# Attention block: scores from two fp32r parts with two heads side by side in 64-row halves, and dense work there in the same halves over three PSUM banks

## The chip, the cores and the metric

The kernel runs on one core of a Trainium2 chip. The metric is device microseconds of one execution. Engines are named as the profile names them: PE multiplies matrices, PEld loads its weights, ACT, DVE and POOL work element by element, and SP issues nearly all DMAs.

## The reference, cut

One transformer block on 2048 tokens of width 640: a layer norm, then attention (32 heads of 20, a sliding window of 256 keys) and a gated GELU MLP (1728 wide) side by side, summed with the input.

```python
xn = _layernorm(x)
q, k, v = qkv[0], qkv[1], qkv[2]            # qkv = xn @ wqkv, H = 32, Dh = 20
scores = einsum("bhqd,bhkd->bhqk", q, k) * Dh ** -0.5
mask = (i - j >= 0) & (i - j < 256)
p = softmax(where(mask, scores, -1e9)); o = einsum("bhqk,bhkd->bhqd", p, v)
A = o @ wo
B = (gelu(xn @ w_gate) * (xn @ w_up)) @ w_down
return x + A + B
```

## The kernel before

Weights and normalised inputs are split into a rounded part and a remainder, both fp32r, and a dense product is three passes over the five 128-row slices of the 640: 15 matmuls into one PSUM bank (`dense_steps`). The tokens are four chunks of 512.

**Prelude** (to some 60 us): layer norm, transposes, V of half the heads, and Q and K of the first tile of 128 columns. **Attention** (to some 565 us) is 32 units: `u` is a group of four heads and a chunk. **Then** come the rest of the gate and up products and the output products, in code that the change hardly touches.

A Q or K product of 128 columns and 512 tokens is one job of 15 matmuls. `save_qk` takes its bank apart into three bf16 parts: ACT rounds, DVE subtracts, ACT rounds the rest, POOL subtracts again, and `store` puts the tile `pt` into DRAM (`qd`, `kd`), in two or three DMAs of SP, one for each head group that the tile touches. `load_stack` brings a unit's parts back as six blocks of 20 rows for each head, 124 rows with four more that hold the row maximum and ones: `qs` and `ks`, 12 DMAs a unit.

A unit in attention has 14 slots (`NS`), in program order: 
- `max_pair`, eight a unit: scores of one block of queries for two heads, in bf16, on 60 rows in each of the two 64-row halves of the array and 32 output columns; DVE takes the row maximum. They come two at a time at the slots in `BURSTS` and behind the AV product.
- `max_end`: the negated maximum is turned (`ps_n`), ACT copies it to `mr`, and a DMA puts it into two rows of the query stack.
- `exp_piece`, twelve a unit (`SCORES`): for one head, the scores of up to 512 columns from the 124 rows, then one ACT exponential. `clear` masks them on POOL.
- `av_unit` at slot 0 of the next unit: probabilities times V in fp32, in 64-row halves and 32 columns, into two banks that ACT copies and POOL adds. `od` and `sd` take the result, five DMAs.
- Between them `pull_fill` draws 34.05 dense matmuls a unit (`RATE`) from `filler`: Q and K jobs of the tiles 1 to 4, V of the other heads, and gate and up products. Q and K jobs come in the units 0 to 10 and again in 18 to 21.

In this stage the order on PE, ACT, DVE, POOL and SP is the order of the code (`manual_schedule`). Work at later slots goes through `defer(n, fn)`, which puts it n slots on; `late` puts DVE work behind the slot's other work. SP issues its DMAs one by one, and each waits on one of eight semaphores in turn, that is, for the DMA eight places earlier to have landed. Eight PSUM banks: two for dense jobs (`psd`), six in a ring for scores, maxima and AV (`psr`).

Of the kernel before, what the change touches and what calls it, by code (L numbers as in the profile page):

```python
# [19 lines left out]
C = 512  # L20
# [9 lines left out]
QROWS = 64 + SR  # L30
NS = 14
BURSTS = 0, 4, 8
SCORES = {2: range(0, 3), 4: range(3, 5), 6: range(5, 7), 8: range(7, 9), 10: range(9, 12)}
# [6 lines left out]
KSLOT = 9  # L40
# [30 lines left out]
def block_kernel(ctx, tc, x, wqk, wv, wgu, wdo, wdl, out):  # L71
# [18 lines left out]
    qd = [dram.tile([NG, 3, 4 * DH, C], BF, name=f"qd{c}") for c in range(NC)]  # L90
    kd = [dram.tile([NG, 3, 4 * DH, C], BF, name=f"kd{c}") for c in range(NC)]
# [159 lines left out]
    def save_qk(t, c, ps):  # L251
        pt = qkp.tile([128, 3, C], BF, name="pt", tag="pt")
        r = qkp.tile([128, C], F32, name="r", tag="r", bufs=1)
        dst = (qd if t < 5 else kd)[c]
        h, l = (2, 0) if t < 5 else (0, 2)

        def lower():
            nc.scalar.activation(pt[:, 1, :], r, AF.Copy)  # L258
            nc.gpsimd.tensor_tensor(out=pt[:, l, :], in0=r, in1=pt[:, 1, :], op=OP.subtract)  # L259
            defer(2, store)  # L260

        def store():
            a, end = t % 5 * 128, t % 5 * 128 + 128
            while a < end:
                g, b = divmod(a, 4 * DH)
                n = min(4 * DH - b, end - a)
                p = n - end + a + 128
                nc.sync.dma_start(dst[g, :, b:b + n, :].rearrange("p m t -> m p t"), pt[p - n:p])
                a += n
            done.add((t, c))  # L270

        def middle():
            nc.vector.tensor_tensor(out=r, in0=ps, in1=pt[:, h, :], op=OP.subtract)
            defer(lag(), lower)

        def upper():
            nc.scalar.activation(pt[:, h, :], ps, AF.Copy)
            late(middle)

        defer(1, upper)  # L280
# [57 lines left out]
    NQ, NK = 3, 4  # L338
    qs = [st1.tile([128, 4, C], BF, name=f"qs{i}") for i in range(NQ)]
    ks = [st1.tile([128, 4, C], BF, name=f"ks{i}") for i in range(NK)]  # L340
    nms = [st1.tile([128, 4, 2, 4, 4], BF, name=f"nm{i}") for i in range(2)]
# [82 lines left out]
    with tc.tile_pool(name="lp", bufs=1, side="right") as lp:  # L424
# [15 lines left out]
        ones = lp.tile([4, 2 * C], BF, name="ones")  # L440
        nc.gpsimd.memset(ones, 0.0)
        nc.gpsimd.memset(ones[0:2], 1.0)
        for i in range(NK):
            for j in (0, 2):
                nc.sync.dma_start(ks[i][SR:64, j:j + 2].rearrange("p j t -> p (j t)"), ones)
        for c in range(1, NC):
# [13 lines left out]
            if c == 1:  # L460
                for i in range(NQ):
                    for j in (0, 2):
                        nc.sync.dma_start(qs[i][SR + 2:64, j:j + 2].rearrange("p j t -> p (j t)"), ones[2:4])
# [18 lines left out]
    psr = pp.enter_context(tc.tile_pool(name="psr", bufs=6, space=PSUM, reuse_waits="tile"))  # L482
    ap = pr.enter_context(tc.tile_pool(name="ap", bufs=2, side="right", reuse_waits="tile"))

    def load_stack(u, which=(0, 1)):
        g, c = divmod(u, NC)
        for m in range(80 * g // 128, (80 * g + 79) // 128 + 1):
            assert all((m + 5 * i, c) in done for i in which), (u, m)

        for i in which:  # L490
            dst, src, top, again = ((qs[u % NQ], qd[c], 1, 2), (ks[u % NK], kd[c], 0, 0))[i]
            for j in (0, 2):
                for p, part, n in ((j * 32, top, 2), (j * 32 + 2 * DH, again, 1), (64 - j * 32, 0, 3)):
                    nc.sync.dma_start(dst[p:p + DH * n, j:j + 2].rearrange("p j t -> p (j t)"),
                                      src[g, part:part + n].rearrange("s (d j) t -> (s d) (j t)",
                                                                      j=4)[:, j * C:(j + 2) * C])
# [6 lines left out]
    def max_pair(u, i):  # L503
        g, c = divmod(u, NC)
        jj, b = divmod(i, 4)
        q, k = qs[u % NQ], ks[u % NK]
# [5 lines left out]
        for h in range(4):  # L512
# [3 lines left out]
            if k0 < 0:  # L516
                parts.append((0, -k0, ks[(u - 1) % NK], C + k0, C) if c else (0, -k0, k, 0, None))
            todo += [(i_, h, q0, *part) for i_, part in enumerate(sorted(parts, key=lambda p: p[1] - p[0]))]
        for _, h, q0, lo, hi, kt, k0, k1 in sorted(todo, key=lambda p: p[:2]):
            for r, ps in enumerate(pss):  # L520
                rows, j = slice(64 * r, 64 * r + SR), 2 * r + jj
                keys = kt[rows, j, k0:k1] if k1 else kt[rows, j, 0:1].to_broadcast([SR, hi])
                nc.tensor.matmul(ps[32 * h:32 * h + 32, lo:hi], q[rows, j, q0:q0 + 32], keys,  # L523
# [6 lines left out]
        if i == 7:  # L530
# [4 lines left out]
            def negate():  # L535
                nc.vector.tensor_scalar(nm[:, 0, 0], mx, -1.0, None, op0=OP.mult)
                nc.vector.scalar_tensor_tensor(nm[:, 0, 1], mx, -1.0, nm[:, 0, 0], op0=OP.mult, op1=OP.subtract)
# [3 lines left out]
    def max_end(u):  # L541
        nm = maxes.pop(u)
        ps = bank("ps_n")
        nc.tensor.matmul(ps[:, 0:128], nm.rearrange("p z a j b -> p (z a j b)"), identb, start=True, stop=True)
        mr = ap.tile([32, 128], BF, name="mr", tag="mr")
        nc.scalar.activation(mr, ps[0:32, 0:128], AF.Copy)
        late(lambda: nc.scalar.dma_start(qs[u % NQ][SR:SR + 2].rearrange("p j t -> p (j t)"), mr))

    def pieces(c):
# [4 lines left out]
        return X, Z, Y  # L554
# [13 lines left out]
    def exp_piece(u, s):  # L568
        g, c = divmod(u, NC)
        bi, j = divmod(s, 4)  # L570
        todo = pieces(c)[bi]
        q = qs[u % NQ]
# [5 lines left out]
        ps = bank("ps_e")  # L578
        for kb, col, q0, n in sorted(todo, key=lambda p: p[3]):
            k = ks[(u - (kb < 4 * c)) % NK]  # L580
# [943 lines left out]
```

## Time and profile before

| | |
|---|---|
| time, three runs | 1043.07, 1043.63 (median), 1044.32 us |
| the profiled execution, its span | 1044.52 us, 1042.8 us |
| PE, DVE, ACT, POOL busy | 99%, 70%, 51%, 36% of the span |
| DMA moved | 158.95 MB, 152 GB/s on the mean |
| granted clock of PE | 0.999 |

All rows shown below are of this one execution. Matmuls overlap, so busy shares of PE say little of how fast it goes; distances between starts do. The start of the AV product marks a unit. SP's instructions are all issues and waits: the length of a row there is the time that SP took for the issue, not the transfer.

### The profile page before, as it was taken

Reading aid. Unit: us, or ns where it says so; the run is one execution under the profiler, and the core shown is the slowest. Engines: PE = TensorE matmul, PEld = TensorE weight load, DVE = VectorE, ACT = ScalarE, POOL = GpSimd, SP = SyncE. Lnnn points to the kernel's source line nnn. Section 1 sums busy time; section 2 is a strip of 40 time slices with the busy share of each in tenths; the row PEclk is TensorE's granted clock in tenths of the full one; section 3 lists DMA queues with packets and bytes.
Section 4 is the critical chain, followed back from the end, with each engine's and each line's share of the span. In section 5 each row is a group of like instructions: output and inputs, shape, how many; then the busy total and the mean of one; then the engine's idle time right before and its main releaser. Section 6 shows DMA issues by size and latency. Waiting matters only on the chain.

```text
span 1042.8 us, 28733 instructions
## 1 busy us (share of the span) xinstructions
PE 1027.2 (99%) x10941; PEld 853.3 (82%) x10941; DVE 728.3 (70%) x2007; ACT 527.8 (51%) x1120; POOL 377.1 (36%) x543
## 2 busy tenths in 40 slices
PE   8999999999999999999999999999999999999998
PEld 7987776677678876777677888888888999999998
DVE  8845666666665566776653778777556879888887
ACT  4444667666666667666666522323234544333332
POOL 5221778876565568665755111110110000000000
PEclk9999999999999999999999999999999999999999
DMA  5652465555333354444332557666216874443342
GB/s 201 190 148 62 134 180 162 171 158 175 104 105 93 94 168 135 150 126 142 100 92 91 190 187 248 232 240 243 102 66 248 257 234 137 136 128 119 119 137 92
DMA packets 105203, 158.95 MB, mean 152 GB/s; under 512 B 15420, under 2 KB 60092, under 8 KB 105064
## 3 DMA queue, kind: packets, MB, share of 16 engines
q1 hardware_dynamic: 102680, 150.95, 45.9%
q10 hardware_dynamic: 2384, 6.16, 1.9%
q8 instruction: 86, 1.41, 0.6%
q14 instruction: 53, 0.43, 0.1%
HBM read 101.78 MB, written 54.92 MB: 150 GB/s over the span
## 4 chain that ended last, share of the span: by engine, by line
PE 84%; DVE 7%; DMA 4%; ACT 2%; issue 1%; SPq 1%; POOL 0%; ACTq 0%; DVEq 0%
PE ps_d L110 22%; PE ps_g L968 21%; PE ps L1235 14%; PE ps_e L582 8%; PE ps_v L110 7%; PE ps_o L622 6%; PE ps_m L523 4%; DVE junk L527 2%; PE ps_g L110 1%; DVE ss L1073 1%; DMA qs<-qd 1%; DVE at L1073 1%; PE ps_t L181 1%; DVE wt L1073 1%; DMA stg<-wtd 1%
## 5 line engine op out<-in xcount | busy, mean ns | idle before, releaser
L527 DVE CUSTOM_DVE_ANT_0 junk<-ps_m,mask 128x288 bf16<-128x288 f32 (+2 forms) x512 | 227.8, 445 | 140.3 <-PE ps_m L523 82.5
L584 ACT ACTIVATE P<-ps_e 128x512 f32<-128x512 f32 (+2 forms) x384 | 195.5, 574 | 60.0 <-PE ps_e L582 58.9
L1235 PE MATMUL ps<-wb,at 128*128 128x320 f32 x999 | 156.4, 310 | 0.8 <-DVE xr L1261 0.7
L1235 PEld LDWEIGHTS ps<-wb,at 128*128 128x128 f32 x999 | 148.9, 188 | 1.4 <-issue 0.9
L595 POOL TENSOR_SCALAR_AFFINE_SELECT P<-P 128x512 f32<-128x512 f32 x128 | 83.8, 656 | 93.5 <-ACT P L584 92.2
L582 PE MATMUL ps_e<-qs,ks 124*128 124x128 bf16 (+2 forms) x704 | 107.3, 277 | 2.1 <-DVE mx L527 2.0
L110 PE MATMUL ps_d<-xh,wql 128*128 128x512 f32 x350 | 105.3, 410 | 0.0
L110 PE MATMUL ps_d<-xl,wqh 128*128 128x512 f32 x350 | 105.3, 410 | 0.0
L110 PE MATMUL ps_d<-xh,wqh 128*128 128x512 f32 x350 | 105.3, 411 | 0.0
L1235 PE MATMUL ps<-wt,at 128*128 128x320 f32 x552 | 89.3, 310 | 0.4 <-DVE u L1073 0.4
L582 PEld LDWEIGHTS <-ks 124*128 124x128 bf16 x704 | 51.5, 98 | 41.0 <-issue 24.0
L1235 PEld LDWEIGHTS ps<-wt,at 128*128 128x128 f32 x552 | 82.9, 188 | 0.9 <-DVE u L1073 0.9
L1189 ACT ACTIVATE at<-ss 128x512 fp32r<-128x512 f32 x59 | 37.3, 633 | 91.4 <-DVE ss L1073 91.4
L622 PE MATMUL ps_o<-P,v 64*32 64x320 f32 (+5 forms) x2816 | 82.0, 348 | 0.0
L103 POOL TENSOR_TENSOR wql<-wr,wqh 128x640 fp32r<-128x640 f32 x11 | 17.6, 1605 | 173.9 <-PE ps_g L968 129.4
L598 POOL TENSOR_SCALAR_AFFINE_SELECT P<-P 128x512 f32<-128x512 f32 x112 | 71.3, 647 | 16.9 <-ACT P L584 16.8
L622 PEld LDWEIGHTS ps_o<-P,v 64*32 64x32 f32 x2816 | 66.7, 106 | 9.8 <-DVE mx L527 4.5
L110 PEld LDWEIGHTS ps_d<-xh,wql 128*128 128x128 f32 x350 | 63.9, 189 | 12.8 <-issue 1.6
L110 PEld LDWEIGHTS ps_d<-xh,wqh 128*128 128x128 f32 x350 | 63.3, 189 | 12.6 <-issue 0.9
L110 PEld LDWEIGHTS ps_d<-xl,wqh 128*128 128x128 f32 x350 | 63.6, 189 | 12.1 <-issue 1.5
L523 PE MATMUL ps_m<-ks,qs 60*32 60x96 bf16 (+5 forms) x3008 | 64.9, 244 | 3.8 <-DVE mx L527 2.3
L259 POOL TENSOR_TENSOR pt<-r,pt 128x512 bf16<-128x512 f32 x40 | 46.8, 1170 | 57.4 <-ACT pt L258 57.4
(196 smaller groups left out, 1889.4 us busy)
## 6 DMA issues: line engine op xcount, KB each, us to landing
hr<-hd SPq DMA_DIRECT2D x104, 128.0 KB
hd<-he SPq DMA_DIRECT2D x50, 256.0 KB
wr<-wgu SPq DMA_DIRECT2D x27, 320.0 KB
qs<-qd SPq DMA_DIRECT2D x64, 120.0 KB
ks<-kd SPq DMA_DIRECT2D x64, 120.0 KB
xi<-x SPq DMA_DIRECT2D x16, 320.0 KB
qs<-qd SPq DMA_DIRECT2D x64, 80.0 KB
ks<-kd SPq DMA_DIRECT2D x64, 80.0 KB
```

Of the source, the lines that this page charges most:

```text
L110: nc.tensor.matmul(ps, a(k), b(k), start=n == 0, stop=n == 3 * nk - 1)
L259: nc.gpsimd.tensor_tensor(out=pt[:, l, :], in0=r, in1=pt[:, 1, :], op=OP.subtract)
L523: nc.tensor.matmul(ps[32 * h:32 * h + 32, lo:hi], q[rows, j, q0:q0 + 32], keys, start=True, stop=True, tile_position=(64 * r, 32 * h))
L527: nc.vector.tensor_tensor_reduce(out=junk[:, 0:n], in0=ps[:, 0:n], in1=mask[:, 288 - n:288], scale=1.0, scalar=NEG, op0=OP.add, op1=OP.max ...
L582: nc.tensor.matmul(ps[:, col:col + n], k[0:QROWS, j, kc:kc + 128], q[0:QROWS, j, q0:q0 + n], start=True, stop=True)
L584: nc.scalar.activation(pt[:, j, lo:hi], ps[:, lo:hi], AF.Exp, scale=SCALE)
L595: nc.gpsimd.affine_select(out=a, in_=a, pattern=[[0, 4], [1, 128]], compare_op=OP.is_ge, fill=0.0, base=0, channel_multiplier=-1)
L598: nc.gpsimd.affine_select(out=a, in_=a, pattern=[[0, 4], [-1, 128]], compare_op=OP.is_ge, fill=0.0, base=-1, channel_multiplier=1)
L622: nc.tensor.matmul(halves[h][32 * j:32 * j + 32, q0:q0 + n], v[rows, w0_:w0_ + 32], pts[u, bi][rows, j, col:col + n], start=i == 0, stop=i ...
L968: nc.tensor.matmul(ps, i, j, start=first and n == 0, stop=n == len(work) - 1, skip_group_check=True)
L1189: nc.scalar.activation(hi[:, 3:7], s, AF.Copy)
L1235: nc.tensor.matmul(ps[bank][:, 0:HD], *work[bank][j], start=bank not in begun, stop=final[p, bank] == n and j == len(work[bank]) - 1, skip ...
```

## The change

**Scores.** `save_qk` leaves two fp32r parts (tile `pe`: rounded, remainder) and two bf16 parts (tile `pm`), and both go to DRAM. A unit has two pairs of stacks: `qe`, `ke` in fp32r for the exponentials (three products of 20 rows and two rows for the maximum: 62 rows a head), `qm`, `km` in bf16 for the maxima (60 rows). Head `2r + j` lies in the half `r`, so one `exp_piece` multiplies two heads, one in each half, into two banks; there are six a unit, and 16 stack DMAs where 12 were. The maximum goes in by two DMAs on SP (one on ACT before).

**Dense work in attention.** A job is now 15 matmuls over the upper 64 rows, then 15 over the lower, into the same bank. `halves` runs the upper ones of one job beside the lower ones of the job before, over three banks (`psd`, `psd3`; the ring has five). Before a job's lower matmuls begin, a `nop` on ACT waits for its last upper one, and PE waits for the `nop`; six steps lie between (`HALF_LAG`).

**AV** uses all 128 rows and 32 columns and one bank, so one copy by ACT and no addition on POOL.

```diff
-BURSTS = 0, 4, 8
-SCORES = {2: range(0, 3), 4: range(3, 5), 6: range(5, 7), 8: range(7, 9), 10: range(9, 12)}
+BURSTS = 4, 8, 12
+SCORES = {1: (0,), 3: (1,), 5: (2,), 7: (3,), 9: (4,), 10: (5,)}
+HALF_LAG = 6
...
+    def soon(fn, *a):
+        if now[0] is None or now[0] < 0:
+            fn(*a)
+        else:
+            at(now[0] + 1, fn, *a)
...
     def save_qk(t, c, ps):
-        pt = qkp.tile([128, 3, C], BF, name="pt", tag="pt")
...
+        pe = qkp.tile([128, 2, C], F32R, name="pe", tag="pe")
+        pm = qkp.tile([128, 2, C], BF, name="pm", tag="pm")
...
-                nc.sync.dma_start(dst[g, :, b:b + n, :].rearrange("p m t -> m p t"), pt[p - n:p])
+                for d, part in zip(dst, (pe.bitcast(F32), pm)):
+                    nc.sync.dma_start(d[c][g, :, b:b + n, :].rearrange("p m t -> m p t"), part[p - n:p])
...
+        def third():
+            nc.gpsimd.tensor_tensor(out=pm[:, 1, :], in0=pe[:, 0, :].bitcast(F32), in1=pm[:, 0, :], op=OP.subtract)
+            defer(2, store)
+
+        def lower():
+            nc.vector.tensor_tensor(out=pe[:, 1, :], in0=ps, in1=pe[:, 0, :].bitcast(F32), op=OP.subtract)
 
         def upper():
-            nc.scalar.activation(pt[:, h, :], ps, AF.Copy)
-            late(middle)
-
+            nc.scalar.activation(pe[:, 0, :], ps, AF.Copy)
+            nc.scalar.activation(pm[:, 0, :], ps, AF.Copy)
+            late(lower)
+            defer(1, third)
+
+        soon(upper)
         defer(1, upper)
...
-        ps = bank("ps_e")
+        pss = [bank("ps_e") for _ in range(2)]
         for kb, col, q0, n in sorted(todo, key=lambda p: p[3]):
...
+            for r, ps in enumerate(pss):
+                rows = slice(64 * r, 64 * r + SR + 2)
+                nc.tensor.matmul(ps[:, col:col + n], k[rows, j, kc:kc + 128], q[rows, j, q0:q0 + n],
+                                 start=True, stop=True, tile_position=(64 * r, 0))
...
+                if n == len(up.steps):
+                    nop = nc.scalar.nop()
+                    tc.add_manual_dep(nop.ins, ins.ins.name, SYNC, reason="halves")
+                    second.append([up, nop.ins.name, HALF_LAG])
...
-                if u + 3 < NU and i in (KSLOT, 12):
-                    load_stack(u + 3, (int(i == KSLOT),))
+                if i == 1 and u + 2 < NU:
+                    load_stack(u + 2, 1)
+                if i == 2 and u + 1 < NU:
+                    load_stack(u + 1, 0)
```

`save_qk` ends in two calls for `upper`, the new one through `soon` and the old one through `defer`. From unit 0 on both put it one slot on; before that `soon` calls it at once. So all that hangs on `upper` stands in the program twice for each Q or K job.

On SP, before the change, at the end of unit 7's stretch: a Q job's three stores, and the stores of the attention result.

```order
L268 DMA qd_85<-pt 16x3x512 [waits DMAHW3_49,Pool_49]
L268 DMA qd_85<-pt 80x3x512 [waits DMAHW4_49]
L268 DMA qd_85<-pt 32x3x512 [waits DMAHW5_49]
L632 DMA od_95<-ob 20x512 [waits DMAHW6_49,Pool_49]
```

On SP, with the change, in the stretch of unit 6: the eight stores of one Q job with two pieces, a weight load, and the two DMAs of the maximum (`mr`). DMAHW0 to DMAHW7 are the eight semaphores of landed DMAs.

```order
L270 DMA qd_87<-pe 64x2x512 [waits DMAHW2_49,DVE_49,Activation_49]
L270 DMA qd_91<-pm 64x2x512 [waits DMAHW3_49,Activation_49,Pool_49]
L270 DMA qd_87<-pe 64x2x512 [waits DMAHW4_49]
L270 DMA qd_91<-pm 64x2x512 [waits DMAHW5_49]
L270 DMA qd_87<-pe 64x2x512 [waits DMAHW6_49,DMAHW2_49]
L270 DMA qd_91<-pm 64x2x512 [waits DMAHW7_49,DMAHW3_49]
L270 DMA qd_87<-pe 64x2x512 [waits DMAHW4_49,DMAHW0_49]
L270 DMA qd_91<-pm 64x2x512 [waits DMAHW5_49,DMAHW1_49]
L302 DMA wvr<-wv 128x320
L561 DMA qe_175<-mr 2x8x128 [waits Activation_49]
```

Where a two-piece job had two stores it now has eight; the last four write what the first four wrote, and each waits for the landing of the one four places earlier. The maximum of the next unit stands behind them.

On ACT, with the change, behind one AV product: the four exponentials of two score pieces, and then one job's bank is copied.

```order
L604 ACTIVATE P<-ps_e 128x512 [waits PE_49,Pool_49]
L604 ACTIVATE P<-ps_e 128x512 [waits PE_49] x3
L282 ACTIVATE pe<-ps_d 128x512 [waits DMAHW3_49,DMAHW1_49,DMAHW5_49,DVE_49,DMAHW7_49,PE_49,Pool_49]
L283 ACTIVATE pm<-ps_d 128x512 [waits DMAHW4_49,DMAHW6_49,DMAHW2_49,DMAHW0_49]
L282 ACTIVATE pe<-ps_d 128x512 [waits Activation_49]
L283 ACTIVATE pm<-ps_d 128x512 [waits Activation_49]
```

Four copies stand where `pt` had two activations (L277, L258); DVE and POOL have two subtractions each where they had one.

On PE, with the change, behind a burst of maxima: matmuls of two dense jobs alternate, one job's lower half (weights `wqh`, its first waits for ACT's `nop`) beside the next job's upper half (`wql`), and the scores of two heads.

```order
L731 MATMUL ps_d<-xh_77,wql 128x512
L731 MATMUL ps_d<-xh_77,wqh 128x512 [waits Activation_sequencer_49]
L731 MATMUL ps_d<-xh_77,wql 128x512
L731 MATMUL ps_d<-xh_77,wqh 128x512
L601 MATMUL ps_e<-qe_175,ke_177 128x128 [waits DMAHW3_49,DMAHW4_49,DMAHW0_49,DVE_49]
L601 MATMUL ps_e<-qe_175,ke_177 128x128 [waits DMAHW5_49,DMAHW6_49,DMAHW1_49,DVE_49]
L601 MATMUL ps_e<-qe_175,ke_178 128x384 [waits DMAHW7_49]
L601 MATMUL ps_e<-qe_175,ke_178 128x384 [waits DMAHW2_49]
```

The first scores of a unit wait for the landing of the stack loads and of the two DMAs from `mr`, all of them SP's now; before, ACT issued the one from `mr`.

SP's DMAs, counted in the two programs between one unit's `sd` store and the next:

| stretch | DMAs before | of them Q/K stores, stacks | DMAs after | of them Q/K stores, stacks, `mr` |
|---|---|---|---|---|
| units 1 to 10 | 247 | 55, 120 | 471 | 216, 160, 20 |
| units 18 to 21 | 91 | 16, 48 | 165 | 64, 64, 8 |
| units 11 to 17 | 130 | 0, 84 | 173 | 0, 112, 14 |

More of the change, by code (lines that the diff above doesn't have):

```diff
@@ L439, in block_kernel @@
         v0 = v0[0]
[L440 to L445, printed above, removed]
+        ones = lp.tile([2, C], F32, name="ones")
+        nc.gpsimd.memset(ones, 1.0)
+        for k in ke:
+            for r in (0, 64):
+                for j in range(2):
+                    nc.sync.dma_start(k[r + SR:r + SR + 2, j].bitcast(F32), ones)
         for c in range(1, NC):
@@ L505, in max_pair @@
         jj, b = divmod(i, 4)
[L506 removed]
+        q, k = qm[u % NQ], km[u % NK]
         if i == 0:
@@ L707, in filler @@
     def filler():
-        yield from proj_qk(0, w0, 3)
-        yield from proj_qk(5, w5, 3)
-        ws = [split_qk(raw) for raw in raws1]
+        yield from qk_job(0, w0, 3)
+        yield from qk_job(5, w5, 3)
+        ws = []
+        for t in range(8 + VEARLY, 12):
+            yield from v_job(v0, t)
+            ws.append(split_qk(raws1[len(ws)]))
         v1 = []
@@ L798, in block_kernel @@
     stream = ((u, i) for u in range(NU) for i in range(8))
-    fill = filler()
+    fill = halves(filler())
     debt = [0.0]
```

230 lines of the change are left out of this document (134 added, 96 removed).

## The prediction

> **What bounds the kernel now.** I read the page first, for the engine that is never idle and the chain that ended last.
>
> ```profile
> span 1042.8 us, 28733 instructions
> PE 1027.2 (99%) x10941; PEld 853.3 (82%) x10941; DVE 728.3 (70%) x2007; ACT 527.8 (51%) x1120; POOL 377.1 (36%) x543
> PE 84%; DVE 7%; DMA 4%; ACT 2%; issue 1%; SPq 1%; POOL 0%; ACTq 0%; DVEq 0%
> L622 PE MATMUL ps_o<-P,v 64*32 64x320 f32 (+5 forms) x2816 | 82.0, 348 | 0.0
> ```
>
> PE carries 84% of the chain. The L622 row shows that half-array matmuls do run side by side: 2816 of 348 ns are 980 us of length in 82.0 us. Only attention changes, so the chain of that window comes next, with the starts of four AV products, which mark units 0, 10, 17 and 21.
>
> ```profile
> by line: PE ps_d L110 42.1%; PE ps_e L582 17.5%; PE ps_o L622 12.3%; PE ps_m L523 8.3%; PE ps_v L110 7.8%; DVE junk L527 3.5%; DMA qs<-qd 2.7%; issue 1.5%; SPq L494 0.9%; SPq L268 0.6%; ACT P L584 0.5%; PE ps_n L544 0.4%; DVE nm L536 0.3%;
> ...
> 182.59 3.90 DMA qs<-qd
> ```
> ```profile
> 105.14 2.33 PE ps_o L622 x48
> ...
> 255.92 2.85 PE ps_o L622 x63
> ```
> ```profile
> 359.10 2.21 PE ps_o L622 x59
> 373.64 2.21 PE ps_o L622 x61
> ...
> 417.40 2.21 PE ps_o L622 x61
> ```
>
> Units 1 to 10 take 150.8 us, 18 to 21 take 58.3 us, a unit without Q and K jobs some 14.6 us (359.10 to 373.64). From 105 to 562.4 us the scores hold 17.5% of the chain, 80 us or 2.58 us for each of 31 units; AV 12.3%. But stack loads and SP's issues are on the chain too, so the last views are the windows and SP's own rows.
>
> ```profile
> core 0: us, PE busy (x) PEld busy (x) DVE busy (x) ACT busy (x) POOL busy (x), PEclk, DMA share, GB/s
> 105.10:255.90 150.80, 147.99 (x2384) 105.92 (x2375) 96.46 (x365) 102.67 (x206) 117.28 (x169) 1.00 0.56 161
> 359.10:417.40 58.30, 58.22 (x966) 42.02 (x963) 38.09 (x145) 39.85 (x81) 42.98 (x63) 1.00 0.49 141
> ```
> ```profile
> 236.23 1.31 SPq L268 DMA_DIRECT2D kd<-pt  x3
> 237.65 2.22 SPq L494 DMA_DIRECT2D ks<-kd  x6
> 239.96 1.33 SPq L268 DMA_DIRECT2D qd<-pt  x3
> 241.39 0.59 SPq L494 DMA_DIRECT2D qs<-qd  x1
> ```
> ```profile
> 229.99 1.42 SPq L632 DMA_DIRECT2D od<-ob  x4
> 231.46 0.50 SPq L633 DMA_DIRECT2D sd<-ob  x1
> ```
>
> Start to start, SP takes 1.42/3 = 0.47 us for a Q/K store, 2.31/6 = 0.385 for a stack load, 1.47/4 = 0.37 for an `od`, about 0.55 for an `sd`; I take 0.43, between them, for the others. The 247 DMAs of units 1 to 10 (55 stores, 120 loads, 40, 10, 22 others) then cost 26 + 46 + 15 + 5 + 9 = 101 us of 150.8. SP has a third of its time left, no more.
>
> **The change part by part.**
>
> *The doubled `upper`, and the stacks: SP.* Units 1 to 10 now have 471 DMAs: 216 stores, 160 loads, 20 from `mr`, 50 of AV, 25 others. An fp32r load and one from `mr` are not in the trace; both go by the load's 0.385. That is 102 + 62 + 8 + 20 + 11 = 203 us, more than the ten units take now. The queue is in order, and the next unit's scores wait for the two DMAs from `mr` that stand behind the stores: PE will wait there once a unit. Then the second store of a piece waits for the first to have landed, four to six stores (1.9 to 2.8 us) behind it. The load at 182.59 held the chain for 3.9 us; at that landing time each of some 22 jobs waits 1 to 2 us more, at 2 us it waits for nothing. I take 0.6 us: 14 us. Sum 217, **+66 us**. The nearest rows for the store's own price bound it:
>
> ```profile
> L268 SPq DMA_DIRECT2D qd<-pt x48: 316/436/1520, 22.9 to 413.9; - x48
> ```
>
> Some 40 ns lie between two issues (0.473 a store against the median 0.436). At the shortest, 0.316 + 0.04, it is 179 us without any landing wait (+28); at 0.52, a tenth above the two stretches, and with 2 us for each job 258 (+107). I stay by the two stretches above, which are what SP does back to back.
>
> Units 18 to 21: 64 stores, 64 loads, 8, 16, 4, 9: 30 + 25 + 3 + 6 + 2 + 4 = 70 us and 0.6 for each of 8 jobs, 75 against 58.3: **+17 us**, bounds +5 and +28. Units 11 to 17 with 25 DMAs, some 10 us a unit, stay PE's.
>
> *The doubled `upper`: the engines.*
>
> ```profile
> L277 ACT ACTIVATE pt<-ps_d x40: 577/597/632, 18.6 to 412.0; 128x512 bf16<-128x512 f32 x40
> L273 DVE TENSOR_TENSOR r<-ps_d,pt x40: 637/690/694, 20.3 to 414.8; 128x512 f32<-128x512 f32 x40
> ...
> L259 POOL TENSOR_TENSOR pt<-r,pt x40: 1157/1167/1332, 21.7 to 417.8; 128x512 bf16<-128x512 f32 x40
> ```
>
> A job had two ACT operations, one of DVE, one of POOL; it has four, two, two. With 2.25 jobs a unit this adds 2.7 us to ACT's 10.3 (102.67/10), 1.6 to DVE's 9.6 and 2.6 to POOL's 11.7; AV gives back one ACT copy and POOL's addition. All stay under 15 us a unit, SP's 21.7 hides them: nothing. Were SP not late, POOL would be next.
>
> *Scores and dense work.*
>
> ```profile
> 40.36 8.79 PE ps_v L110 x60
> 49.16 6.83 PE ps_d L110 x30
> ```
>
> An fp32r matmul takes 8.79/60 = 146.5 ns for 320 columns and 6.83/30 = 227.7 for 512: 0.423 ns a column and 11 ns each. Two heads side by side then take 11 + 11 + 512 × 0.423 = 239 ns for a piece, six pieces 1.43 us a unit against 2.58: −1.1. A 128-column matmul whose weights do not arrive in its 65 ns may give 0.15 of that back: −0.95 a unit. No row shows a dense matmul in halves. Two concurrent halves cost what the whole one costs, 227.7, or at best the bare columns, 217: 34.05 × 11 ns = −0.4 a unit; at worst they take turns (a rival below). I take 0, the nearest row.
>
> *AV and bursts.* AV had windows of up to 320 columns in halves, 1344 columns after one another in a full unit; now 1536: 1536/1344 × 2.21 = +0.3 us. Bursts of maxima now begin four times a unit from dense work, not three, and AV stands in a form of its own.
>
> ```profile
> 300.85 0.46 PE L110 MATMUL ps_v<-wvh,xh 128*128 128x320 f32 x2
> 301.23 0.45 PE L523 MATMUL ps_m<-ks,qs 60*32 60x32 bf16 x32
> ...
> 304.22 0.70 PE L110 MATMUL ps_v<-wvh,xh 128*128 128x320 f32 x3
> 304.76 0.74 PE L110 MATMUL ps_v<-wvh,xl 128*128 128x320 f32 x4
> ```
>
> Two matmuls before the burst should last 0.29 us; it starts 0.09 late. Behind it three take 0.54, 0.10 too long. So a burst costs 0.2, between 0 (if halves to halves is free, then −0.6 for the three that went) and 0.3. Behind this row stands a rule of the Trainium skill, "TensorEngine Tiling (Array Packing)", section "Key Properties": changing the tiling mode drains the array. The 0.09 and 0.10 agree; by it the change from AV's form to the maxima's drains once more, and the sum would be 17 × 0.2 = 3 us longer.
>
> A unit that PE bounds: −0.95 + 0.3 + 0.2 = −0.45, between −1.1 − 0.4 + 0.3 − 0.6 = −1.8 and −0.3; I take −0.6, as part of the 0.4 is likely. 17 such units (0, 11 to 17, 22 to 30): **−10 us**.
>
> *The staggering itself.* At the start 15 + 6 upper matmuls run alone, at the end as many lower ones: 42 × 0.228/2 = **+5 us**. The `nop` asks PE for nothing if ACT reaches it within six steps, 1.4 us; the exponentials are 574 ns each, so two may stand before it. Taken as nothing.
>
> *Prelude.* Six jobs do all twice, with 36 more DMAs, and the next chunk's loads of x stand behind the stores. PE is the chain there and the loads are early: **+3 us**, between 0 and 10.
>
> **Sum**: 66 + 17 − 10 + 5 + 3 = +81. The profiled execution took 1044.5 us, 1.7 more than its span; its time gives 1125.5, and the median shown is 0.9 under it: 1125.
>
> **Rivals.**
>
> *The DMA engines, not SP's issue.*
>
> ```profile
> qd<-pt SPq DMA_DIRECT2D x16, 240.0 KB
> ...
> qs<-qd SPq DMA_DIRECT2D x64, 40.0 KB
> ```
>
> 80 rows are 240 KB, a job 384 KB; twice two fp32 and two bf16 parts are 1536. Stacks go from 960 to 1440 KB a unit. Units 1 to 10 move 24.3 MB (161 GB/s × 150.8 us) and would move 56. At the full rate of that window, 161/0.56 = 288 GB/s, that is 195 us (+44), units 18 to 21 68 (+10): 1096. For it: near SP's 203. Against: SP's figure is higher. A rule of the Trainium skill, "DMA: Bandwidth & Descriptors", section "Issuing engines are not separate DMA queues", says that a sequencer's time for issuing is usually small beside the DMA itself; by it this rival is the case. The rows say otherwise: 101 us of issuing beside 0.56 × 150.8 = 84 us of transfers.
>
> *The `nop`.* If ACT is two exponentials late at each of 2.27 jobs, PE waits 2.27 × 1.15 = 2.6 us in 17 units that SP does not bound: +44, 1170. For it: ACT is in order, 70% busy; against: six steps of lead.
>
> *The halves take turns.* Then dense work costs 34.05 × 0.228 = 7.8 us more a unit; SP's wait covers that in 14 units, 17 pay 7.8: 1125 + 133 = 1258. Against: the L622 row.
>
> *Faster.* SP or the engines issue and move faster than any row, and PE's gain decides everywhere: at −1.2 a unit, the middle of −0.6 and −1.8, 31 units and the 8 of the last two parts give −29, 1015. It needs 47 DMAs and 5.6 MB in a unit of 13.4 us, 0.285 us a DMA and 418 GB/s. Against: the shortest issue is 0.316 for a store, and the fullest stretch gives 345 GB/s:
>
> ```profile
> 640.00:700.00 60.00, 60.00 (x267) 49.69 (x266) 47.18 (x80) 17.41 (x34) 8.96 (x6) 1.00 0.69 238
> ```
>
> **How the numbers follow.** SP 0.62, DMA engines 0.15, the `nop` 0.08, taking turns 0.04, faster 0.08, no change 0.03. 0.2% or 2 us is what a measurement can tell. The range 1068 to 1185 takes in SP's bounds nearly to their ends (1125 − 38 − 12, 1125 + 41 + 11 and the rest), the DMA engines and the `nop`; turns and faster lie outside. Slower 0.89.
>
> **What would show it.** In units 1 to 10 SP issues without a pause, PE waits once a unit for a DMA `qe<-mr`, and units take 20 us or more; units 11 to 17 take about 14. Wrong: a PE wait on `nop` in those, dense starts over 250 ns apart a pair, or units 1 to 10 under 18 us.

## The result, and the profile after

| | before | after |
|---|---|---|
| time, median (4 runs each, same chip) | 1043.35 us | 1303.14 us (1297.14 to 1308.19) |
| ratio, 95% interval | 1 | 1.2486 (1.2432 to 1.2541) |
| the profiled execution, its span | 1044.52, 1042.8 us | 1308.19, 1306.5 us |
| granted clock of PE | 0.999 | 0.926 |

The forecast was 1125 us, 1068 to 1185. The direction was right, the size was not: 264 us more of span, where 81 had been worked out.

The page of the changed kernel, the lines that answer to those of before; `PEclk` is the granted clock in tenths, for 40 slices of the span.

```profile
span 1306.5 us, 29772 instructions
PE 1125.5 (86%) x10885; PEld 903.8 (69%) x10885; DVE 752.0 (58%) x2047; ACT 552.9 (42%) x1200; POOL 379.3 (29%) x550
...
PEclk9886897778877889998889999999999999999999
...
PE 58%; DMA 14%; SPq 8%; DVE 8%; ACT 5%; issue 5%; POOL 2%; DVEq 0%; ACTq 0%; POOLq 0%
```

PE is no longer always busy (86%), and its share of the chain fell from 84% to 58%; DMA and SP's queue have 22% of it. The clock column tells where: most of its digits below 9 lie in the first half, at the start and where Q and K jobs run, and it is 9, its highest digit, elsewhere.

The starts of AV products in the chain of the changed kernel, which end units 10, 11, 18 and 22 (counted from 0), from three stretches of it; then the windows between such marks.

```profile
446.55 2.73 PE ps_o L629 x48
```
```profile
473.47 2.73 PE ps_o L629 x48
...
585.26 2.73 PE ps_o L629 x48
```
```profile
685.17 2.73 PE ps_o L629 x48
```
```profile
core 0: us, PE busy (x) PEld busy (x) DVE busy (x) ACT busy (x) POOL busy (x), PEclk, DMA share, GB/s
60.00:166.80 106.80, 83.46 (x731) 67.64 (x729) 37.69 (x120) 32.66 (x98) 27.38 (x35) 0.81 0.51 151
166.80:446.50 279.70, 187.83 (x2304) 127.65 (x2302) 109.49 (x386) 118.86 (x250) 130.31 (x179) 0.82 0.67 191
473.40:585.20 111.80, 107.48 (x1783) 79.86 (x1781) 63.12 (x248) 62.16 (x180) 52.31 (x90) 1.00 0.41 129
585.20:685.10 99.90, 73.15 (x924) 49.47 (x922) 43.12 (x154) 45.03 (x95) 46.79 (x67) 0.85 0.71 205
826.60:1306.50 479.90, 475.23 (x2696) 431.86 (x2695) 371.09 (x716) 177.65 (x323) 25.65 (x18) 1.00 0.52 171
```

The first AV product starts at 166.8 us for 105.0 before (+62). Units 1 to 10 take 279.7 us for 150.8 (+129), unit 11 26.9 for 15.1 (+12), 12 to 18, without Q and K jobs, 111.8 for 102.6 (+9), 19 to 22 99.9 for 58.3 (+42), 23 to 31 141.5 for 130.6 (+11), and all behind the last AV product 479.9 for 480.4. The sum is the 264 us. In the two stretches with Q and K jobs PE is busy for 187.83 of 279.70 and 73.15 of 99.90 us. These stretches run up to a unit behind the program's Q and K jobs (units 0 to 10 and 18 to 21), since SP still issues stores of them then: 9 in unit 11, 12 in unit 22.

One such unit, the one that begins with the AV product at 271.85 and with 34.9 us the longest of the ten: first SP's queue, then PE, in order of time (start, length, line, and in brackets the wait ahead), then the windows ahead of PE's pause, in it and behind it.

```profile
266.49 3.88 SPq L637 DMA_DIRECT2D od<-ob  x4
270.42 0.57 SPq L638 DMA_DIRECT2D sd<-ob  x1
271.09 0.61 SPq L270 DMA_DIRECT2D kd<-pe  x1
...
277.93 0.57 SPq L270 DMA_DIRECT2D kd<-pm  x1
278.62 0.57 SPq L270 DMA_DIRECT2D qd<-pe  x1
...
284.27 0.57 SPq L270 DMA_DIRECT2D qd<-pm  x1
284.90 0.60 SPq L302 DMA_DIRECT2D wvr<-wv  x1
285.56 1.41 SPq L561 DMA_DIRECT2D qe<-mr  x2
```
```profile
274.31 0.50 PE L731 MATMUL ps_d<-xl,wqh 64*128 64x512 f32 x1
...
274.65 0.39 PE L731 MATMUL ps_d<-xl,wqh 64*128 64x512 f32 x1
...
274.88 0.39 PE L731 MATMUL ps_d<-xl,wqh 64*128 64x512 f32 x1
274.88 0.39 PE L731 MATMUL ps_d<-xh,wql 64*128 64x512 f32 x1
287.95 1.24 PE L601 MATMUL ps_e<-qe,ke 62*128 62x128 f32 x4 [12.68 <-issue]
...
289.34 0.62 PE L731 MATMUL ps_d<-xl,wqh 64*128 64x512 f32 x1
...
289.76 0.62 PE L731 MATMUL ps_d<-xh,wqh 64*128 64x512 f32 x1
```
```profile
271.00:275.00 4.00, 4.00 (x78) 2.03 (x76) 1.60 (x8) 0.00 (x0) 0.00 (x0) 1.00 0.68 166
...
281.00:284.00 3.00, 0.00 (x0) 0.00 (x0) 1.19 (x2) 2.07 (x5) 1.16 (x2) 0.50 0.95 254
...
288.00:292.00 4.00, 4.00 (x20) 3.84 (x22) 0.00 (x0) 1.90 (x4) 0.00 (x0) 0.50 0.86 221
```

The two DMAs of the maximum stand behind sixteen stores of two jobs, eight of them the second time; the first scores start a microsecond behind them, after PE has stood for 12.68 us. It is the longest of 19 pauses of over 1 us in these ten units, 79 us together. ACT stood in this unit as well, for 10.69 us until 280.41: its copy into `pe`, a tile with two buffers, waits for stores out of it to land. PE's last wait is the one for the maximum; a third buffer was not tried. From 271.09 to 284.90 us are 13.81 for sixteen stores, 0.86 each. Behind the pause the same dense matmuls take 0.62 us and start 0.42 apart, ahead of it 0.39 and 0.23: the granted clock has fallen from 1.00 to 0.50. The Trainium skill, "TensorE: Matmul & The Clock Gate", Part 1, says that an idle array is taken to half its clock and back after about 3.4 us of work; the rows agree with the fall to half. The 0.82 of the ten units is the mean over many such pauses. The clock was still full when this pause began, so here the fall follows from the wait and is not its cause.

### The profile page after: what moved, and what is told of

Its sections match the earlier page's. It is cut to its first block, busy times and chain, and to the rows that moved or that the text cites. A ratio compares the mean times of both kernels' runs of the same rounds, so it can differ in the third digit from the quotient of the medians.

```text
span 1306.5 us, 29772 instructions
## 1 busy us (share of the span) xinstructions
PE 1125.5 (86%) x10885; PEld 903.8 (69%) x10885; DVE 752.0 (58%) x2047; ACT 552.9 (42%) x1200; POOL 379.3 (29%) x550
## 4 chain that ended last, share of the span: by engine, by line
PE 58%; DMA 14%; SPq 8%; DVE 8%; ACT 5%; issue 5%; POOL 2%; DVEq 0%; ACTq 0%; POOLq 0%
PE ps L1313 14%; PE ps_g L1046 14%; PE ps_d L731 12%; SPq L270 4%; PE ps_o L629 4%; PE ps_e L601 4%; DMA ke<-kd 3%; PE ps_v L731 3%; SPq L500 3%; PE ps_m L529 3%; DVE junk L533 2%; DMA kd<-pm 2%; DMA qd<-pm 2%; ACT pm L283 2%; PE ps_v L111 2%
## 5 line engine op out<-in xcount | busy, mean ns | idle before, releaser
L731 PE MATMUL ps_d<-xl,wqh 64*128 64x512 f32 x660 | 222.9, 442 | 0.0
L731 PE MATMUL ps_d<-xh,wqh 64*128 64x512 f32 x660 | 220.0, 445 | 3.3 <-DVE pe L279 3.3
L731 PE MATMUL ps_d<-xh,wql 64*128 64x512 f32 x660 | 222.6, 443 | 0.0
L601 PE MATMUL ps_e<-qe,ke 62*128 62x128 f32 (+2 forms) x704 | 117.4, 350 | 96.2 <-DMA qe<-mr 46.3
L601 PEld LDWEIGHTS ps_e<-qe,ke 62*128 62x128 f32 x704 | 89.9, 211 | 121.7 <-issue 77.2
L275 POOL TENSOR_TENSOR pm<-pe,pm 128x512 bf16<-128x512 f32 x80 | 93.2, 1166 | 221.0 <-ACT pm L283 152.0
L731 PEld LDWEIGHTS ps_d<-xh,wqh 64*128 64x128 f32 x660 | 129.6, 211 | 15.9 <-issue 4.6
L731 PEld LDWEIGHTS ps_d<-xh,wql 64*128 64x128 f32 x660 | 130.9, 211 | 13.0 <-issue 5.0
L731 PEld LDWEIGHTS ps_d<-xl,wqh 64*128 64x128 f32 x660 | 130.6, 210 | 11.5 <-issue 2.8
L629 PE MATMUL ps_o<-P,v 128*32 128x384 f32 (+2 forms) x1408 | 84.3, 386 | 0.0
```

The lines of the kernel that those rows point to most:

```text
L275: nc.gpsimd.tensor_tensor(out=pm[:, 1, :], in0=pe[:, 0, :].bitcast(F32), in1=pm[:, 0, :], op=OP.subtract)
L601: nc.tensor.matmul(ps[:, col:col + n], k[rows, j, kc:kc + 128], q[rows, j, q0:q0 + n], start=True, stop=True, tile_position=(64 * r, 0))
L629: nc.tensor.matmul(o[32 * j:32 * j + 32, q0:q0 + n], v[:, w0_:w0_ + 32], pt[:, j, col:col + n], start=i == 0, stop=i == len(todo) - 1, ski ...
L731: return nc.tensor.matmul(self.ps[:, 0:self.n], a[p, k, self.rows], b[p, k, self.cols], start=r == 0 and i == 0, stop=r == 1 and i == len( ...
```

## The experiments

Theory D: the doubled `upper` costs nearly all. Its rivals: the doubled work of ACT, DVE and POOL (E) and not the DMAs; bytes and not the number of DMAs; the new form of scores, AV and dense work itself (R). All kernels below are edits of the changed one, unless said otherwise. The stages in the table are distances between starts of AV products, from each kernel's trace; SP's DMAs are those issued in units 1 to 11, "us each" those units' time over that number. The times of the changed kernel, x1, c3 and b1 are medians of 4, 4, 4 and 6 runs; the others ran once, so differences of a few us between them say nothing (x1's four runs lie within 4.6 us, those of the changed kernel within 11).

| kernel | time | first AV | 1-11, a unit | SP's DMAs | us each | 12-18, a unit | 19-22, a unit |
|---|---|---|---|---|---|---|---|
| before | 1043.4 | 105.0 | 15.08 | 269 | 0.62 | 14.66 | 14.58 |
| after | 1303.1 | 166.8 | 27.87 | 507 | 0.60 | 15.97 | 24.97 |
| x1_once | 1159.1 | 123.7 | 20.72 | 391 | 0.58 | 15.83 | 18.62 |
| x2_engines_twice | 1179.0 | 142.1 | 20.83 | 391 | 0.59 | 15.96 | 18.43 |
| x3_stores_twice | 1273.8 | 142.1 | 27.06 | 507 | 0.59 | 15.81 | 25.20 |
| x4_stores_elsewhere | 1270.8 | 141.6 | 27.05 | 508 | 0.59 | 15.81 | 24.38 |
| x5_stores_small | 1249.4 | 135.3 | 26.28 | 507 | 0.57 | 15.84 | 23.03 |
| z1_one_result_store | 1140.4 | 123.6 | 18.29 | 347 | 0.58 | 15.73 | 16.93 |
| c1_turn_one_store | 1139.6 | 122.7 | 18.38 | 347 | 0.58 | 15.71 | 16.80 |
| p1_loads_on_pool | 1139.7 | 121.9 | 19.75 | 348 | 0.62 | 15.87 | 17.08 |
| c3_turn_store_pool | 1132.8 | 124.5 | 17.92 | 303 | 0.65 | 15.74 | 16.35 |
| m1_max_on_act | 1167.1 | 124.6 | 21.05 | 360 | 0.64 | 15.97 | 18.95 |
| y2_stacks_on_act | 1215.3 | 127.4 | 20.78 | 308 | 0.74 | 19.36 | 21.82 |
| y3_best | 1226.4 | 129.2 | 20.82 | 283 | 0.81 | 19.94 | 21.42 |
| w1_dense_whole | 1168.0 | 115.4 | 20.54 | 394 | 0.57 | 17.21 | 18.25 |
| v1_av_halves | 1162.0 | 124.8 | 20.74 | 391 | 0.58 | 16.07 | 18.65 |
| c2_all_whole | 1160.4 | 115.5 | 18.65 | 349 | 0.59 | 17.11 | 17.38 |
| y1_turn_whole | 1154.7 | 122.1 | 20.56 | 391 | 0.58 | 15.80 | 18.43 |
| b2_before_twice | 1141.8 | 132.3 | 20.06 | 330 | 0.67 | 14.79 | 18.38 |
| b1_before_one_store | 1060.5 | 104.9 | 14.99 | 226 | 0.73 | 14.65 | 14.63 |

### One `upper`

```diff
         soon(upper)
-        defer(1, upper)
```

> One `upper` a job instead of two; all else as changed. If the doubling is what costs (theory D), the time falls to about 1085 us, 1075 to 1095: the time before, plus 1.2 us for each of 31 units, which is what the changed kernel's units without Q and K jobs take more than before (15.4 to 16.5 us against some 14.6), plus some 5 us of start. If the forecast's small terms hold in all units it is 1040 us. If the new form of scores, AV and dense work is what costs (rival R), the time stays over 1200 us.

It took 1159.11 us (1157.59 to 1162.19, 4 runs), ratio 1.1109 (1.108 to 1.1137). So 144 of the 260 us are the doubling's (theory D), and 115 stay with the form (R); the 1085 us of D fails too, since I had carried the units without Q and K jobs over to those with them.

```profile
core 0: us, PE busy (x) PEld busy (x) DVE busy (x) ACT busy (x) POOL busy (x), PEclk, DMA share, GB/s
...
123.70:331.00 207.30, 169.79 (x2300) 113.57 (x2298) 95.78 (x364) 97.39 (x206) 105.27 (x158) 0.92 0.61 179
367.90:462.40 94.50, 91.67 (x1552) 69.11 (x1550) 50.51 (x209) 53.12 (x159) 41.14 (x69) 1.00 0.43 131
```

In these windows of it PE still waits in units 1 to 10 (169.79 of 207.30 us) and hardly in those without Q and K jobs (91.67 of 94.50). Even one set of stores leaves SP more than it had.

### Engines, stores, landings, bytes

The doubled half each way: all of `upper` twice but one `store` (x2); one `upper` and `store` twice, into one place (x3), the second into a place of its own (x4), and that with 128 of the 512 columns (x5).

```diff
 # x2
-        soon(upper)
-        defer(1, upper)
+        soon(upper, False)
+        defer(1, upper, True)        # True: third goes on to store
 # x3, x4, x5: one upper
-        defer(1, upper)
 # x3
             defer(2, store)
+            defer(2, store)
 # x4
+            defer(2, store, qx if t < 5 else kx)
 # x5
+                    w = C if dst in (qd, kd) else 128
```

> Both calls of `upper` stay, but only the second one stores: ACT, DVE and POOL do all twice, the DMAs are those of one call. If SP's issues and the landings of the stores are what costs, it lies within 25 us of the kernel with one `upper`, near 1100 us. If the doubled work of the engines costs (rival E), it stays at 1250 us or more.

> One `upper` a job, and `store` twice into the same place: ACT, DVE and POOL do everything once, the DMAs are those of the changed kernel and each second one waits for the landing of the first. If SP and the landings cost (forecast), units 1 to 10 take 25 us and more and the whole 1250 to 1300 us. If the engines cost (rival E), it is near 1100 us.

> As the kernel that stores twice, but the second time into a place of its own that nobody reads: the same number of issues and bytes, and no store waits for another to land. If the waits for landings make the difference between SP's pure issue time and what was seen, units 1 to 10 take 5 to 8 us less each than with both stores into one place, some 20 to 22 us, and the whole about 1180 us. If the issues or the bytes alone cost, the time is that of the kernel that stores twice, within 20 us.

> One `upper`; the second stores go to a place of their own and carry 128 of the 512 columns: as many DMAs and rows as where both stores are whole (1270.8 us), a quarter of the second ones' bytes. If the number of DMAs that SP has to issue costs, it stays at 1240 us or more. If the bytes on the DMA engines cost, a quarter of the 112 us between 1159 and 1271 is left: about 1187 us.

Measured: 1178.97, 1273.78, 1270.83 and 1249.42 us. In attention the doubled work of the engines costs nothing (20.83 us a unit for 20.72), and the doubled stores everything (27.06). Their landings cost next to nothing: with a place of its own for the second store the units are as long (27.05), so the wait of a second store for the first is not the term, which leaves the second of x4's two cases. Three quarters of the second stores' bytes taken away give 0.8 us a unit and 21 us in all; their number, with a quarter of the bytes and as many rows, keeps 90 of the 112 us. In the windows of x3 and x5:

```profile
60.00:142.10 82.10, 67.34 (x676) 53.47 (x674) 31.92 (x113) 24.04 (x72) 19.18 (x28) 0.85 0.59 171
142.10:413.60 271.50, 185.04 (x2300) 126.56 (x2298) 93.26 (x364) 97.96 (x206) 104.73 (x157) 0.81 0.69 196
```
```profile
135.30:399.90 264.60, 185.16 (x2303) 126.20 (x2301) 93.12 (x364) 97.92 (x206) 105.11 (x157) 0.81 0.54 155
```

The DMA engines go from 0.69 to 0.54 busy and from 196 to 155 GB/s, and the ten units from 271.5 to 264.6 us. The issue of a second store gets shorter too (`qx<-pe`, median, from 0.64 us in x4 to 0.44 in x5), so the length of an issue is not free of the bytes behind it.

Ahead of the first AV product both halves of the doubling cost, and as much: 123.7 becomes 142.1 with the engines' and 142.1 with the stores'; together 166.8. PE is idle for 15 and 14 of 82 us in the windows of x3, above, and of x2:

```profile
60.00:142.10 82.10, 67.92 (x659) 54.67 (x657) 28.17 (x97) 27.66 (x79) 20.30 (x21) 0.81 0.37 110
```

### Fewer DMAs for SP, by three ways

With one `upper`: one result store of 128 rows for five (z1); the same with one product that turns the maxima (c1); the bf16 loads on ACT (y2); the maximum's two DMAs on ACT (m1); the four bf16 query loads on POOL (p1), and that on c1 (c3). The edits of z1, c1 and c3 also read the result from its new place behind attention.

```diff
 # z1, c1, c3
-            for j in range(4):
-                nc.sync.dma_start(od[c].rearrange("(d h) t -> h d t", h=H)[4 * g + j], ob[32 * j:32 * j + DH, :])
-            nc.sync.dma_start(sd[c][4 * g:4 * g + 4, :], ob[DH::32, :])
+            nc.sync.dma_start(o2[c][128 * g:128 * g + 128], ob)
 # y2
-                    nc.sync.dma_start(to[64 * r + p:64 * r + p + DH * n].rearrange("p j t -> p (j t)"),
+                    (nc.sync, nc.scalar)[i].dma_start(to[64 * r + p:64 * r + p + DH * n].rearrange("p j t -> p (j t)"),
 # m1
-                nc.sync.dma_start(qe[u % NQ][64 * r + SR:64 * r + SR + 2]      # ...
+                nc.scalar.dma_start(qe[u % NQ][64 * r + SR:64 * r + SR + 2]    # ...
 # p1, c3
-                    nc.sync.dma_start(to[64 * r + p:64 * r + p + DH * n]    # ...
+                    (nc.gpsimd if any(dst is q_ for q_ in qm) else nc.sync).dma_start(to[64 * r + p:64 * r + p + DH * n]    # ...
```

> One `upper`, and the result of a unit goes to DRAM in one DMA of 128 rows where it took five, with about as many bytes (256 KB for 176); the reads of it much later take a few DMAs more. SP has 32 DMAs a unit with Q and K jobs where it had 36. If SP's queue bounds these units, by 0.58 us a DMA, they take 2 us less each: units 1 to 10 some 18.5 us, the whole about 1132 us. If bytes bound them, the time stays at 1159 or rises.

> One `upper`, the maxima turned by one product into one bank, one result store a unit. The sum of the two edits alone: 4.5 us and whatever the one store gives, by SP's queue 27 us: about 1128 us.

> One `upper`, and the eight bf16 stack loads of a unit are issued by ACT, so that SP has 8 of its 36 DMAs of a unit with Q and K jobs less; bytes and numbers of DMAs as a whole are the same. If SP's queue bounds units 1 to 10, they go from 20.7 us to about 17, and the whole to some 1115 us. If the DMA engines bound them, the time stays within 8 us of 1159. If ACT's own order makes it late, units without Q and K jobs get longer than 15.7 us.

> One `upper`, and the two DMAs of the maximum are issued by ACT as the one before the change was. By the count alone (34 DMAs a unit for 36, 0.58 us each) units 1 to 11 go from 20.7 to 19.5 us, the whole to about 1142. If these two standing behind the stores is what costs (order in the queue, not length), units 1 to 11 fall to 17 us or less, the whole under 1115.

> One `upper`, and the four bf16 query loads of a unit are issued by POOL: 36 DMAs in all as before, 32 of them on SP. If SP's queue bounds units 1 to 11 (0.58 us for each of its DMAs), they take 18.4 us for 20.7 as with one result store, the whole about 1125 us. If the DMAs as a whole bound them, or their landings, they stay at 20.7. If POOL gets late by issuing, units without Q and K jobs get longer than 15.8 us as with the loads on ACT.

> One `upper`, the maxima turned in one product, one result store a unit, and the four bf16 query loads on POOL: 28 DMAs a unit on SP. By 0.58 us a DMA units 1 to 11 take 16.2 us, near what PE needs (15.7), the whole about 1112 us, still slower than before the change. If something else than SP's queue bounds them, they stay above 18 us.

Taken away, four DMAs a unit are worth 2.4 us, as the rate of 0.58 us a DMA says (z1: 18.29 for 20.72, though the one store has 128 rows for 84; in all 1140.42 us and not 1132, because the product behind attention takes 17 us longer when it reads the new place). The turn in one product adds nothing to that (c1: 1139.62, expected about 1128). Given to another engine they are worth less. POOL, in the rows of p1, issues a load in 0.517 us and has room for it:

```profile
L499 POOL DMA_DIRECT2D qm<-qd x128: 510/517/683, 60.2 to 616.0; - x128
L499 SPq DMA_DIRECT2D km<-kd x128: 272/331/1286, 61.8 to 616.6; - x128
```

but the units fell by 1.0 us and not by 2.4, and the issues that stayed on SP in units 1 to 11 grew from 0.445 us on the mean (x1, without `qm`) to 0.469. So the rate seems to be SP's for one part and that of all DMAs together for another. The Trainium skill, "DMA: Bandwidth & Descriptors", "Issuing engines are not separate DMA queues", says that issuing on several engines saves only the sequencer's time; here it saved 1.0 of 2.4 us. On ACT nothing is gained at all. SP's waits from 100 to 380 us of m1:

```profile
SPq L636 <- DMA qe<-mr: 15.2, 8, 3.0
...
SPq L637 <- DMA qe<-mr: 6.1, 3, 4.8
SPq L499 <- DMA qe<-mr: 4.3, 1, 4.3
```

ACT issues the maximum when its own order lets it, and SP, whose later DMAs wait on the same eight semaphores, now waits for these landings: what was issue time is waiting, 67 us in units 1 to 11 for x1's 45. It also answers whether the two DMAs cost by standing behind the stores: without them there the units stay at 21.05 us. y2 shows the same on ACT's side, with 19.4 us in units that had been 15.8: its expectation's third case. y3 joins the edits of y1 (below), y2 and m1. It was expected at 1090 us by SP's queue or within 15 us of 1159 by the DMA engines, and took 1226.41: neither.

Counted over all engines that issue, units 1 to 11 have 391 DMAs in x1, 382 in m1, 396 in y2, 393 in y3 and 392 in p1, and take 217 to 232 us in all five; they have 347 in z1, c1 and c3, and take 197 to 202. That is 0.55 to 0.61 us a DMA, whoever issues it. So the number of DMAs sets the time of these units to within a tenth. That it does so by SP's issuing, and not by something that all DMAs share, is not shown.

c3 took 1132.79 us (1129.93 to 1135.9, 4 runs), ratio 1.0819 (1.0771 to 1.0867): the best of this form, and still slower than before.

### The form of dense work, AV and the turn

With one `upper`: dense jobs of 15 matmuls on all rows in turn (w1), that on c1 (c2), AV as before the change (v1), the maxima turned by one product into one bank (y1).

```diff
 # w1, c2
-    fill = halves(filler())
+    fill = whole(filler())        # a[:, k, rows], b[:, k, cols], one job after another
 # y1
-        pss = [bank("ps_n") for _ in range(2)]
...
+        ps = bank("ps_n")
+        nc.tensor.matmul(ps[:, 0:128], nm, identb, start=True, stop=True)
+        nc.scalar.activation(mr.rearrange("p r t -> p (r t)"), ps[0:32, 0:128], AF.Copy)
```

> One `upper`, and the negated maxima are turned by one product on all 128 rows into one bank, with one copy by ACT, where two products on 64 rows went into two of the ring's five banks. In the units that PE bounds, 0.65 us lie between the turn and the scores behind it; if that is the wait for a bank, some 0.4 us of it go in each of these 17 units: 8 us less, about 1151 us. If it is the wait for something else, nothing changes.

> One `upper`, and the dense jobs in attention are 15 matmuls on all 128 rows again, each into one of the three banks, with no `nop` and no staggering; scores and maxima stay in halves. If dense work in halves costs nothing by itself and saves a change of form at each piece of scores and each burst (10 a unit at 0.2 us), the units that PE bounds get up to 2 us longer than 15.7. If the halves and their banks are what costs, they fall towards 14.6. By both, the 5 us of the staggered start go. The Q and K units, which SP's queue bounds, stay at 20.7 us by my theory.

> The same with dense work on all 128 rows. In the units without Q and K jobs: the one before plus what dense work in whole rows gives or takes there, between 14.6 and 17.5 us a unit; in units 1 to 10, bound by SP's queue, no difference from the one before.

> One `upper`, and AV as in the kernel before: 64-row halves in two banks, two copies by ACT, the sum on POOL. If AV on 128 rows is what makes the units that PE bounds long (2.73 us for 2.21, and two changes of form), units 12 to 18 fall from 15.8 to 15.1 to 15.3 us and the whole to about 1150. If it is not, they stay at 15.8 or more. In units 1 to 11 no difference.

Dense work in halves is a gain: without it units 12 to 18 take 17.21 us for 15.83 (c2: 17.11), though the start is 8 us shorter (115.4 for 123.7). PE's waits ahead of weight loads in these units, first of w1, then of x1 (sum, times, longest, in us):

```profile
PEld L528 <- issue: 5.0, 19, 0.4
PEld ps_v L878 <- issue: 5.0, 25, 0.2
PEld ps_o L628 <- issue: 4.0, 20, 0.4
PEld ps_e L600 <- issue: 3.8, 18, 0.4
```
```profile
PEld L528 <- issue: 7.7, 27, 0.4
PEld ps_o L628 <- issue: 4.6, 24, 0.2
PEld ps_e L600 <- DVE mx L532: 4.2, 8, 1.0
```

Whole dense matmuls beside scores in halves wait 0.2 us ahead of the weights where the form changes, 25 and 18 times in five units (x1's window has six). The Trainium skill, "TensorEngine Tiling (Array Packing)", "Key Properties", says that a change of the tiling mode drains the array; these rows agree. With dense work in halves that price stands only at the bursts and, new, at AV, which is on all rows now: 24 waits of 0.19 us, which the kernel before does not have. Giving AV its halves back takes those away and gains nothing (1162.04 us, 16.07 a unit): in v1's waits another row comes up,

```profile
PE ps_m L528 <- ACT ob L645: 3.5, 6, 0.6
```

maxima that wait until ACT has copied one of the two banks that AV then holds. The turn in one bank (1154.65) leaves these units at 15.80, though PE is idle for only 1.2 of 94.4 us in six of them, for x1's 2.8 of 94.5. So what waits for banks of the ring are worth is not shown; in y1 PE hardly waits.

### The doubling in the kernel before, and one store there

```diff
 # b2, on the kernel before
         defer(1, upper)
+        defer(1, upper)
```

b1 is the kernel before with z1's edit.

> The kernel before with its one call for `upper` written twice: every Q or K job's bank is taken apart and stored twice, 302 DMAs on SP in units 1 to 10 for 247. By 0.58 us a DMA these units take 17.5 us for 15.1 (+24), units 18 to 21 15.5 for 14.6 (+4), the start some 25 us more: about 1096 us. If the queue's rate is a thing of the new form (two fp32 parts, one unit of look-ahead), units 1 to 10 stay near 15.1 us and only the start gets longer: about 1068 us.

> The kernel before with one result store a unit for five: SP has 21 DMAs in units 1 to 10 for 25. PE bounds these units at 14.6 to 15.1 us; what is above 14.6 there can go, 0 to 5 us: 1039 to 1044 us. If the reads of the result behind attention, eight DMAs more, stand in the way there, it gets 1 or 2 us longer instead.

b2 took 1141.76 us, more than either expectation: 98 us, in the start (+27) and in the units with Q and K jobs (20.06 us). SP's rate is not the reason: in units 1 to 10 it issues for only 65% of the time, and waits for the rest, where the changed kernel's SP issues for 84%. Its longest waits from 100 to 380 us:

```profile
SPq L268 <- POOL pt L259: 39.8, 10, 11.3
SPq L268 <- DMA kd<-pt: 20.8, 22, 1.7
SPq L268 <- DMA qd<-pt: 19.3, 18, 2.4
```

Here, where a job has two or three stores, a second store does wait for the first, two or three places ahead, to land, 40 times; in the new form it stands four to six places behind, and x4 took 3 us less than x3, which single runs do not tell from nothing. The doubled work is in the way here too: in units 1 to 10 ACT's second rounding waits for POOL's part of the same `pt` 22 times, 37 us in all, and POOL for ACT 31 times, 26 us. Which of these makes b2's units long was not separated. b1 took 1060.46 us (1059.43 to 1063.09, 6 runs), ratio 1.0144 (1.0115 to 1.0173): 0.5 us less until the last AV product, 17 more behind it. No version here beats the kernel before.

## Why the prediction was wrong

The sum missed some 183 us: 100 in SP's terms (63 in units 1 to 10, 25 in 19 to 22, 12 in unit 11, which I had counted as PE's), 54 in the start, 30 in the units that PE bounds.

*SP's queue bounds the units with Q and K jobs: right that the number of DMAs does, and mis-sized.* The term was 203 us of issuing and 14 of landing waits for units 1 to 10 and their 471 DMAs; summed over SP's rows of the trace, their 465 DMAs took 234 us with the gaps and another 46 us of waits. Of the 31 us, some 25 are the 224 stores, for which I took two quiet stretches of 0.47 us and which take 0.58 on the mean; 6 are the maximum's DMAs, which I priced as a stack load at 0.385:

```profile
L561 SPq DMA_DIRECT2D qe<-mr x64: 610/642/703, 139.1 to 811.1; - x64
```

(minimum, median, maximum in ns). The loads were right at 0.38. The larger part is the waits, 46 us for 14, and they are not those that I priced. SP's longest in units 1 to 10 of the changed kernel that end with a DMA's landing:

```profile
SPq L637 <- DMA qe<-qd: 12.3, 27, 1.2
SPq L638 <- DMA ke<-kd: 8.6, 7, 2.3
...
SPq L270 <- DMA kd<-pe: 4.5, 10, 1.1
SPq L270 <- DMA qd<-pe: 3.3, 11, 0.4
```

A second store's wait for a first is in the last two rows, 8 us. In the first two the store of the result waits for the stack load eight places ahead of it, which does not write what it reads; such waits make 30 of the 46 us, and my sum had put them at nothing without a reason. For units 18 to 21 the same: 75 forecast, 99.9 measured in 19 to 22.

The rate could not be read from the kernel before. There SP's 251 DMAs in these units also come to 0.60 us each, and 0.60 times 471 is 283 us, but that is luck: in the longest of SP's waits there, 15.7 us in 8 times, it waited for POOL's work on `pt`, not for its own queue, and with fewer DMAs in units as long (b1) the same division gives 0.73.

*The doubled work of the engines is hidden: right in attention* (x2), *wrong ahead of it*, where nothing of SP's lies on top: 18 us. *The prelude and the start, +3 and +5: the step that failed most for its size.* They measured +62: 19 of the form (8 of them the halves run alone, by w1), 18 the engines', 18 the stores', 6 of both together. I had called the loads of x early; with the stores ahead of them in SP's queue they are issued until 69 us where it was 33, and PE waits 11.6 us for the layer norm behind them. Of the 62 us 33 are PE's idle time and 29 its longer busy time.

*Units that PE bounds, −0.6 us each: wrong in sign, +1.2 to +1.3.* Dense pairs do run side by side, 0.23 us apart, so that step holds. The scores gave less than I took: they keep PE busy for 3.1 us a unit in x1's window where it was 3.4, for a forecast of −0.95. AV lasts 2.73 us for 2.21, where I had +0.3, and its change of form, 0.77 us a unit (4.6 over six), was missing. That AV is the cause is not shown, since v1 gave its halves back and gained nothing; nor are the banks of the ring that went from six to five, by y1. The cause of this part stays open.

*The rivals.* The DMA engines: against it stands x5 (0.54 busy, and all but 0.8 us as long); but p1 speaks for a share that all DMAs have together, and y2 and m1 do not rule one out. The `nop`: no wait for it appears among PE's in attention. Taking turns: no. *What would show it* was right for 20 us a unit and the wait for `qe<-mr`; "without a pause" and 14 us in units 11 to 17 were not.

The clock was not in the forecast. It made the work behind pauses dearer, in the start too, where it is 0.81 on the mean from 60 to 166.8 us.

## What to carry to other kernels

Price a queue in a stretch where it is the bound, with its waits: here 0.57 to 0.60 us a DMA in the twelve kernels of the new form that leave all to SP, for 0.46 in the forecast. A division of time by DMAs where another engine is the bound says nothing of the queue (0.62 and 0.73 in two kernels that PE bounds). Count DMAs before bytes, and take them away rather than move them to another engine. When a form of matmul changes, count the changes of form on the array and the banks that each piece holds, as well as the columns.

## What the runs showed of the hardware

A DMA that another engine issues is not free of the queue it left: four loads moved to POOL gave 1.0 us a unit where four stores taken away gave 2.4, and the issues that stayed on SP grew from 0.445 to 0.469 us on the mean. A DMA of 2 rows in 8 pieces of 128 (`qe<-mr`) takes 0.64 us to issue, a load of 40 rows 0.33. Pauses of 1 to 13 us bring the granted clock down to 0.82 on the mean of 280 us, in a kernel on one core that had 1.00 there; in the longest it fell to 0.50.
